# Threshold attention and a gelu feed-forward on one core: v in nine-key packets, two pairs' scores computed twice, and a planner that shares the DMA engines

## The chip, the cores and the metric

The kernel runs on one core of a Trainium2 chip. The metric is the device time of one execution in microseconds (us); the time before is the median of three executions, 1317.71 us (1317.33 to 1318.2). Five engines work side by side, each through its own list of instructions in order: TensorE (PE, matrix products, with weight loads listed apart as PEld), VectorE (DVE), ScalarE (ACT), GpSimd (POOL) and SyncE (SP), which here only issues transfers. Sixteen DMA engines move the data. Products are written to PSUM, everything else lives in SBUF; both have 128 partitions.

## The reference

```python
scores = scale * np.matmul(q, k.transpose(0, 1, 3, 2))      # (8, 8, 576, 64) each
thresh = np.max(scores, axis=-1, keepdims=True) - tau
scores = np.where(scores >= thresh, scores, -1000000000.0)
scores = scores - np.max(scores, axis=-1, keepdims=True)
attn = np.exp(scores)
attn = attn / (np.sum(attn, axis=-1, keepdims=True) + 1e-09)
x = np.matmul(attn, v)          # then (B, H, S, D) -> (B*S, H*D) = (4608, 512)
h = x @ w_in                    # w_in (512, 2048)
g = h * (1.0 / (1.0 + np.exp(-1.702 * h)))
out = g @ w_out                 # w_out (2048, 512)
```

Keys may stand in any order, as long as k and v use the same one: maximum, sum and the product with v run over all keys. In the run q, k, v and tau are 4-byte floats, while the weights w_in and w_out arrive as 8-byte floats.

## The kernel before, in words

**Tiling.** The heads of one batch are taken in pairs: batch 0 is pairs 0 to 3, and 32 pairs in all. For a pair, k and q are loaded in 32-wide blocks (`load_qk`, L366), transposed on DVE (`prep`, L477), and multiplied as four 64x64 quarters of the PE array (`scores`, L493). One tile `j` of nine holds 64 keys by 2 heads by 576 queries: keys lie along partitions, with the first half of the queries on partitions 0 to 63 and the second half on 64 to 127. ACT copies each tile from PSUM to SBUF (`keep`, L510); PSUM has three such tiles (`psA`). DVE takes the maximum over keys with a reduction that transposes (`in_groups`, L516, two key tiles at once, the ninth alone: "t" counts these five pieces), folds it over tiles (`over_tiles`, L525) and over the partition blocks less tau (`over_halves`, L536 and L542). The threshold row is then spread over partitions: for pairs in `BY_DMA` through DRAM (`turn_rows` L553, `row_out` L566, `row_in` L575), for pair 2 by a transpose (`spread_max`, L557). DVE subtracts it (`sub`, L580), ACT sends what is below to minus infinity with a very steep Prelu (`mask`, L586) and exponentiates (`exps`, L590). PE multiplies by a block of ones for the sums and by v for the result (`by_values`, L601, tiles `den` and `pv`). Pairs 0 to 4 take their sums on PE (L632), pairs 5 to 7 on DVE (`one_group`, L643 and L647), later ones on DVE with the row sent through DRAM (`turn_sums`, L658). `place_x` (L703) scales `pv` into the input of the feed-forward, and only then is the PSUM tile of `pv` free.

**Weights.** The 8-byte weights come in 32 pieces of 1 MB, by two transfers each that POOL issues (`load_w`, L428 and L429), and are turned into 4-byte floats by `cv_ex` (L439, DVE), `cv_power` (L447, ACT), `cv_frac` (L453 and L457, DVE) and `cv_end` (L465, DVE), 16 pieces of w_in and then 16 of w_out. Room for pieces not yet converted is short: a new load waits for an earlier `cv_end`. The first three pieces wait on POOL (`hold`, L484) for the transposed k of pair 2, the next three for that of pair 3.

**Stages.** Opening: pairs 0 to 3, with scores of pairs 4 and 5, and w_in. Then the first two feed-forward blocks of 256 tokens (`first_blocks`: L758 for hidden products, L764 for the gelu, L740 for the output), with pairs 4 to 9 worked in and w_out converted. Then steady work: feed-forward blocks (L718, L730, L909, L931) with one pair's attention in between; from pair 7 (`JOINT`) on a pair's scores are interleaved tile by tile with the values of the pair two before. A last stretch without attention ends it.

**What sets the order.** No order is written by hand. `task()` records each step with its engine, a cost in us, a rank, the tasks it follows, the buffers it takes and gives back, and a lag until others see it. Ranks are the pair's number plus a bias from a table by function name: `EARLY` for pairs 0 to 3, `SECOND` for 4 to 7, `LATER` for the rest, `CV` for conversions. `run_in_order()` plays the tasks through a heap of events and each engine takes the lowest-ranked task that is ready, so that the costs decide the order in which instructions are emitted. A transfer is a part of the lag of its issuing task there: fixed 10, 3 or 5.2 us and the like, whatever else moves. On the chip an engine keeps the emitted order, and waits where its next instruction is not ready.

Of the kernel before, what the change touches and what calls it, by code (L numbers as in the profile page):

```python
# [10 lines left out]
FP32 = mybir.dt.float32  # L11
# [4 lines left out]
ALU = mybir.AluOpType  # L16
# [14 lines left out]
def kernel(  # L31
# [84 lines left out]
    stop = const.tile([P, 1], FP32, name="stop")  # L116
    shift = const.tile([P, 1], FP32, name="shift")
# [9 lines left out]
    for x in ("raw0", "raw1", "qkT0", "qkT1", "mb"):  # L127
# [6 lines left out]
        "exps": -11.47,  # L134
        "in_groups": 5.75,
        "keep": 10.66,
        "load_qk": -0.27,
        "load_v": 4.86,
        "mask": -2.66,
        "one_group": -15.86,  # L140
        "one_row": 12.67,
        "over_halves": -7.01,
        "over_tiles": -4.01,
        "place_x": -17.11,
        "prep": -11.73,
        "row_in": 20.49,
        "row_out": 4.47,
        "scores_run": 12.45,
        "spread_max": -1.73,
        "spread_sums": 7.14,  # L150
        "sub": 9.27,
        "sums_by_pe": 0.27,
        "sums_in": -9.39,
        "sums_out": 2.13,
        "turn_rows": -12.55,
        "turn_sums": -0.41,
        "values": 14.64,
        "w_sum": 4.11,
        "x_sum": -14.1,
    }  # L160
    SECOND = {
        "exps": -7.29,
        "in_groups": 20.95,
        "keep": 16.67,
        "load_qk": -8.88,
        "load_v": 5.53,
        "mask": 2.36,
        "one_group": 2.55,
        "one_row": -2.71,
        "over_halves": -12.07,  # L170
        "over_tiles": 2.86,
        "place_x": -20.26,
        "prep": 3.49,
        "row_in": -19.42,
        "row_out": -24.08,
        "scores_run": -7.99,
        "spread_max": -3.11,
        "spread_sums": -2.29,
        "sub": 14.98,
        "sums_by_pe": 35.93,  # L180
        "sums_in": 7.43,
        "sums_out": 4.05,
        "turn_rows": -3.84,
        "turn_sums": 4.03,
        "values": 11.79,
        "w_sum": -10.45,
        "x_sum": -10.98,
    }
    LATER = {
        "exps": 2.01,  # L190
        "in_groups": 10.37,
        "keep": -0.02,
        "load_qk": -6.6,
        "load_v": 3.77,
        "mask": 14.79,
        "one_group": 4.78,
        "one_row": -14.98,
        "over_halves": 1.09,
        "over_tiles": -6.27,
        "place_x": -0.34,  # L200
        "prep": 2.34,
        "row_in": 4.02,
        "row_out": 2.64,
        "scores_run": -11.25,
        "spread_max": -9.44,
        "spread_sums": -6.73,
        "sub": 2.14,
        "sums_by_pe": 1.46,
        "sums_in": 3.78,
        "sums_out": 2.16,  # L210
        "turn_rows": 12.26,
        "turn_sums": 0.29,
        "values": -10.38,
        "w_sum": 6.61,
        "x_sum": 6.02,
    }
    CV = {
        "cv_end": -8.05,
        "cv_ex": 2.22,
        "cv_frac": -11.72,  # L220
        "cv_power": -4.72,
        "load_w": -7.79,
    }

    LAG = {"PE": 0.26, "DVE": 0.18, "ACT": 0.22, "POOL": 0.18}

    QUARTERS = ("scores", "scores_run", "values", "sums_by_pe")
# [12 lines left out]
    FIRST, LAST = -9.0, 1000.0  # L240
    need, follows = {}, {}

    def run_in_order():
# [7 lines left out]
        events = [(0.0, 1, i) for i, n in enumerate(left) if n == 0]  # L251
# [3 lines left out]
        mode, held_for = None, None  # L255
        while events:
            now = events[0][0]
            while events and events[0][0] <= now:
                _, kind, i = heapq.heappop(events)
                engine, _, rank, _, _, _, _, give, lag = tasks[i]  # L260
                if kind == 0:
                    busy.discard(engine)
# [1113 lines left out]
```

## Time and profile before

| | us |
|---|---|
| median of three executions | 1317.71 |
| the profiled execution, its own time | 1317.94 |
| span of the profiled execution | 1316.2 |
| PE busy / weight loads | 1260.9 / 975.6 |
| DVE, ACT, POOL busy | 1006.1, 646.6, 249.0 |
| PE busy from 0 to 118 us of the span | 77.0 |
| bytes moved | 102.88 MB in 258819 packets |
| packets under 512 bytes | 233754 |

The span runs from the first to the last recorded instruction. A group of instructions in the profile reads: line, engine, operation, output and inputs by tile name, shapes, count, busy time, mean; tile names such as `arena` cover many buffers that share one allocation. In a list of waits, "PE ps L493 <- DVE arena L477: 15.3, 3, 8.3" says that PE's instructions of line 493 stood idle for 15.3 us in 3 stalls, the longest 8.3, until DVE's line 477 was done. Fp32 products appear as two records each. In the table of stretches each engine has its busy time and, in brackets, its count.

### The profile page before, as it was taken

To read this page: it belongs to the slowest core of one execution; us is meant where nothing else is said; L and a number is where in the kernel's file an instruction comes from. 1 tells how busy PE (TensorE), PEld (TensorE's weight loads), DVE (VectorE), ACT (ScalarE), POOL (GpSimd) and SP (SyncE) were. 2 spreads that over 40 slices of the span, in tenths; PEclk is the share of its full clock that TensorE was granted. 3 is DMA by queue.
4 is the path that set the end of the run, shared out by engine and by line. 5 is a ranking of instruction groups with operands and counts; after the bars stand their busy time and mean duration, and the time that the engine had idled before them with its cause. 6 is when DMAs were issued, how large, how long until landed. Compare 5 with 4: busy or idle time off the path is not lost. (4 is left out here: it accounts for less than half of the span.)

```text
span 1316.2 us, 22807 instructions
## 1 busy us (share of the span) xinstructions
PE 1260.9 (96%) x9128; PEld 975.6 (74%) x9128; DVE 1006.1 (76%) x1610; ACT 646.6 (49%) x830; POOL 249.0 (19%) x291
## 2 busy tenths in 40 slices
PE   5669999999999999999999999999999999999998
PEld 2346864457887777777778888777777778888887
DVE  7989999898888887788777877777888863652642
ACT  4876666576554555555554555454556540210210
POOL 1201211012031211213021303030212117120120
PEclk8879999999999999999999999999999999999999
DMA  8976766545323223212213222323122110000000
GB/s 152 293 189 207 230 207 149 112 77 100 85 55 71 55 55 71 51 50 54 58 42 72 55 71 55 71 55 71 36 55 54 36 46 8 9 1 25 8 0 32
DMA packets 258819, 102.88 MB, mean 78 GB/s; under 512 B 233754, under 2 KB 243994, under 8 KB 258714
## 3 DMA queue, kind: packets, MB, share of 16 engines
q1 hardware_dynamic: 244986, 63.40, 22.4%
q0 software_dynamic: 11360, 37.74, 9.3%
q8 instruction: 71, 1.16, 0.4%
q10 hardware_dynamic: 2368, 0.30, 0.2%
q14 instruction: 34, 0.28, 0.1%
HBM read 87.51 MB, written 9.69 MB: 74 GB/s over the span
## 5 line engine op out<-in xcount | busy, mean ns | idle before, releaser
L516 DVE TRANSPOSE_TENSOR_REDUCE part<-arena 128x36 f32<-128x1152 f32 (+1 forms) x295 | 357.5, 1235 | 41.9 <-ACT arena L510 32.4
L718 PE MATMUL hps<-xT,w_in 128*128 128x256 f32 x1536 | 337.2, 380 | 0.5 <-DVE arena L730 0.4
L718 PEld LDWEIGHTS hps<-xT,w_in 128*128 128x128 f32 x1536 | 290.7, 190 | 45.9 <-issue 5.7
L586 ACT ACTIVATE arena<-arena 128x1152 f32<-128x1152 f32 (+1 forms) x160 | 169.4, 1059 | 144.0 <-DVE arena L580 143.8
L510 ACT COPY arena<-ps 128x576 f32<-128x576 f32 x288 | 170.7, 647 | 115.3 <-PE ps L493 111.9
L580 DVE TENSOR_TENSOR arena<-arena 128x1152 f32<-128x1152 f32 (+1 forms) x158 | 201.1, 1313 | 20.5 <-DMA arena<-row 20.5
L909 PE MATMUL ops<-w_out,arena 128*128 128x256 f32 x896 | 202.4, 380 | 1.8 <-DVE arena L730 1.8
L590 ACT ACTIVATE arena<-arena,shift,scl 128x1152 f32<-128x1152 f32 (+1 forms) x160 | 200.3, 1252 | 4.1
L493 PE MATMUL ps<-arena 64*64 64x288 f32 x2304 | 174.7, 420 | 22.9 <-DVE arena L477 15.3
L909 PEld LDWEIGHTS ops<-w_out,arena 128*128 128x128 f32 x896 | 169.3, 190 | 28.7 <-DVE arena L730 3.1
L875 POOL TENSOR_TENSOR arena<-arena 128x256 f32<-128x256 f32 x56 | 49.7, 888 | 647.1 <-DVE arena L730 543.9
L601 PE MATMUL pv<-arena 64*64 64x288 f32 x2176 | 159.7, 408 | 0.0
L727 ACT ACTIVATE th<-hps 128x512 f32<-128x512 f32 x112 | 66.0, 589 | 186.0 <-PE hps L718 171.8
L909 PE MATMUL ops<-arena 128*128 128x256 f32 x672 | 150.7, 380 | 0.7 <-DVE osb L931 0.7
L493 PEld LDWEIGHTS ps<-arena 64*64 64x64 f32 x2304 | 84.0, 137 | 90.8 <-ACT arena L510 30.4
L909 PEld LDWEIGHTS ops<-arena 128*128 128x128 f32 x672 | 127.1, 190 | 20.4 <-issue 2.2
L601 PEld LDWEIGHTS pv<-arena 64*64 64x64 f32 x2176 | 82.1, 134 | 54.1 <-issue 10.0
L931 DVE SCALAR_TENSOR_TENSOR osb<-ops,osb 128x256 f32<-128x256 f32 x98 | 39.3, 413 | 97.9 <-PE ops L909 90.6
L730 DVE SCALAR_TENSOR_TENSOR arena<-th,hps 128x512 f32<-128x512 f32 x96 | 64.2, 669 | 46.7 <-ACT th L727 46.4
L740 PE MATMUL ops<-w_out,arena 128*128 128x512 f32 x128 | 57.2, 600 | 3.2 <-DVE w_out L465 2.2
L758 PE MATMUL hps<-xT,w_in 128*128 128x256 f32 x256 | 56.4, 381 | 0.0
L888 POOL TENSOR_TENSOR arena<-arena 128x512 f32<-128x512 f32 x28 | 35.6, 1272 | 108.3 <-PE ops L909 108.3
(115 smaller groups left out, 1044.7 us busy)
## 6 DMA issues: line engine op xcount, KB each, us to landing
arena<-in_v_dram SPq DMA_DIRECT2D x128, 144.0 KB
arena<-in_q_dram SPq DMA_DIRECT2D x128, 72.0 KB
out_dram<-osb SPq DMA_DIRECT2D x36, 256.0 KB
arena<-in_k_dram SPq DMA_DIRECT2D x124, 72.0 KB
arena<-row SPq DMA_DIRECT2D x62, 144.0 KB
arena<-row_s SPq DMA_DIRECT2D x48, 144.0 KB
w_out<-in_moe_w_in_dram POOLq DMA_DIRECT2D x12, 512.0 KB, 9.5
arena<-in_moe_w_out_dram POOLq DMA_DIRECT2D x12, 512.0 KB, 6.3
```

The costliest lines, as they stand in the source:

```text
L493: nc.tensor.matmul(ps[ts(c, KT), h, 0:SH], lhsT=mats[n, 1][ts(h, D), ts(j, KT)], rhs=mats[n, 0][ts(h, D), ts(c, SH)], start=True, stop=True,)
L510: nc.scalar.copy(out=sT[n, t][:, u], in_=pss.pop((n, j))[:, :, 0:SH])
L516: nc.vector.tensor_reduce(out=stats[n, op][:, t * 2 * QB : min(2 * t + 2, NK) * QB], in_=sT[n, t].rearrange("p u h (g d) -> p (u h g) d", ...
L580: nc.vector.tensor_tensor(out=s, in0=s, in1=mbs[n].unsqueeze(1).to_broadcast(list(s.shape)), op=ALU.subtract)
L586: nc.scalar.activation(out=s, in_=s, func=AF.Prelu, alpha=STEEP)
L590: nc.scalar.activation(out=s, in_=s, func=AF.Exp, scale=scl, bias=shift)
L601: nc.tensor.matmul(o[c][ts(h, D), 0:SH], lhsT=left(j, h)[ts(c, KT)], rhs=sT[n, t][ts(c, KT), u, h, :], start=(j == 0), stop=(j == NK - 1),)
L718: nc.tensor.matmul(hidden[j][:, ts(f, BLK)], lhsT=w_in[:, c, ds((f * HF + j) * P, P)], rhs=xTs[blk][:, c, :], start=(c == 0), stop=(c == N ...
L727: nc.scalar.activation(out=ths[j], in_=hidden[j], func=AF.Tanh, scale=GELU_SCALE / 2)
L730: nc.vector.scalar_tensor_tensor(out=g[:, :, j, :], in0=two(ths.pop(j)), scalar=1.0, in1=two(hidden.pop(j)), op0=ALU.add, op1=ALU.mult,)
L740: nc.tensor.matmul(acc[i], lhsT=g0[:, j, ts(i, P)], rhs=w_out[:, j, :], start=(j == 0), stop=(j == NFC - 1),)
L909: nc.tensor.matmul(banks[blk][k][:, ts(o, HM)], lhsT=left[:, j, :], rhs=right[:, j, :], start=(j == 0), stop=(j == HF - 1),)
```

## The change

**v.** `load_v` reads nine consecutive keys of v into one partition, so that 64 pieces of 2304 bytes take the place of 576 of 256 bytes in each transfer. Key tile `j` then holds every ninth key. For k, `load_qk` loads the blocks in the order that gives the same set of keys, its pieces keep their 128 bytes.

**Scores twice.** For pairs 2 and 3 (`TWICE`) the copied scores are used for the maximum alone. `over_halves` writes the thresholds with all four partition blocks, `row_blocks` transposes them and multiplies by a mask `own_row`, so that each of 64 partitions has the thresholds of its own queries and zero elsewhere. `again` computes the scores a second time and adds to the same PSUM tile a product of that matrix with `minus`, a block of minus ones. `mask_one` is the Prelu straight from PSUM to SBUF. `sub` and `mask` fall away for these two pairs.

**Sums.** Pairs 5 to 7 send their sums through DRAM as the later ones do (`SUMS_BY_DMA` from 5).

**The planner.** A transfer is a task of its own on one of two movers, `DMS` for what SP and ACT issue and `DMW` for POOL's weights. Where both are busy they share: small packets (kind 0) get 0.055 of the engines, larger ones (kind 1) 0.3, the weights the rest. The biases of all tables are new, and the costs of conversions and of SP's issues are changed. `BY_POOL`, which would give some subtractions to POOL, is empty. Four memsets, a fill by position and their constants stand at the program's start on POOL, ahead of the load of tau.

```diff
-        "exps": -11.47,
-        "in_groups": 5.75,
...
+        "again": -31.04,
+        "exps": -25.04,
+        "in_groups": 37.12,
...
+    MOVERS = ("DMS", "DMW")
+    SHARE = (0.055, 0.3)
+    def transfer(by, time, a, kind=0, give=(), lag=1.7):
+        return task(by, time, FIRST, moved, kind, after=[a], give=give, lag=lag)
...
+        def rates():
+            if len(flow) < 2:
+                return dict.fromkeys(flow, 1.0)
+            x = SHARE[tasks[flow["DMS"][0]][4][0]]
+            return {"DMS": x, "DMW": 1.0 - x}
...
+    TWICE = (2, 3)
+    BY_POOL = {}
...
+                rows = src[b, 2 * hp + h, :, ts(j, 32)]
                 queue.dma_start(
                     out=blocks[ds(64 * h + 32 * j, 32), :, :],
-                    in_=src[b, 2 * hp + h, :, ts(j, 32)].rearrange("(c p) d -> p c d", p=32),
+                    in_=rows.rearrange("(a p t) d -> p t a d", a=2, p=32) if which
+                    else rows.rearrange("(c p) d -> p c d", p=32),
                 )
...
-                    out=t[ts(c, KT), :, h, :],
-                    in_=v[b, 2 * hp + h].rearrange("(j k) d -> k j d", k=KT),
+                    out=t[ts(c, KT), h],
+                    in_=v[b, 2 * hp + h].rearrange("(k j) d -> k j d", k=KT),
...
+        if n in TWICE:
+            for x, y in ((0, 0), (1, 2), (2, 1), (3, 3)):
+                nc.vector.scalar_tensor_tensor(
+                    out=flat[0][ts(y, 32), 0:QB], in0=r[ts(x, 32)], scalar=gap[ts(x, 32)],
+                    in1=o[ts(x, 32)], op0=ALU.subtract, op1=ALU.max,
+                )
+            return
...
+    def row_blocks(n):
+        nc.vector.transpose(out=flat[1], in_=flat[0])
+        mb = home(n, "mb")[:, 0:SH]
+        nc.vector.tensor_tensor(
+            out=mb.rearrange("p (g i) -> p g i", i=32),
+            in0=flat[1].unsqueeze(1).to_broadcast([P, QB // 2, 32]),
+            in1=own_row.unsqueeze(2).to_broadcast([P, QB // 2, 32]), op=ALU.mult,
+        )
+        mbs[n] = mb
+
+    def again(n, j):
+        ps = psA.tile([P, 2, 512], FP32, name="ps", tag="ps")
+        for first in (True, False):
+            for h in range(2):
+                for c in range(2):
+                    if first:
+                        left = mats[n, 1][ts(h, D), ts(j, KT)]
+                        right = mats[n, 0][ts(h, D), ts(c, SH)]
+                    else:
+                        left, right = minus[ts(h, D), c, :], mbs[n][ts(h, D), :]
+                    nc.tensor.matmul(
+                        ps[ts(c, KT), h, 0:SH], lhsT=left, rhs=right, start=first, stop=not first,
+                    )
...
+    def mask_one(n, j):
+        nc.scalar.activation(
+            out=sT[n, j // 2][:, j % 2], in_=pss.pop((n, j))[:, :, 0:SH], func=AF.Prelu, alpha=STEEP
+        )
...
+    nc.gpsimd.memset(minus, 0.0)
+    nc.gpsimd.memset(own_row, 0.0)
+    for x in range(4):
+        nc.gpsimd.memset(minus[ts(x, 32), x % 2, :], -1.0)
+        nc.gpsimd.affine_select(
+            out=own_row[ts(x, 32)], in_=own_row[ts(x, 32)], compare_op=ALU.not_equal, fill=1.0,
+            base=-(QB // 2) * (x // 2), pattern=[[-1, QB // 2]], channel_multiplier=1,
+        )
...
-    BY_PE = 5
-    BY_DMA = (0, 1, *range(3, NP))
-    SUMS_BY_DMA = range(8, NP)
+    SUMS_BY_PE = (0, 1, 2, 3, 4)
+    BY_DMA = (0, 1, *range(4, NP))
+    SUMS_BY_DMA = range(5, NP)
...
-        cost = 3.5 if NPAIR <= n < 2 * NPAIR else 2.0
-        lag = (4.6, 3.0)[n] if n < 2 else 10.0 if n < 2 * NPAIR else 3.0
...
+        lq, lk = (transfer("DMS", 1.45, a, lag=1.7 if n else 3.2) for a in (lq, lk))
...
+            if n in TWICE:
+                for j in range(2 * t, min(2 * t + 2, NK)):
+                    m = task(
+                        "PE", 0.97 * slow, r, again, n, j, after=[m], take=("psA",),
+                        give=own(n, "qkT0", "qkT1", "mb") if j == NK - 1 else (),
+                    )
+                    a = task("ACT", 0.62, r, mask_one, n, j, after=[m] + mx, give=("psA",))
+                ws.append(task("ACT", 0.76 if tail else 1.24, r, exps, n, t, after=[a]))
+                continue
```

## The prediction

> **What bounds the kernel now.** I read the page's first part, then the engines by stretch, then what TensorE waited for.
>
> ```profile
> PE 1260.9 (96%) x9128; PEld 975.6 (74%) x9128; DVE 1006.1 (76%) x1610; ACT 646.6 (49%) x830; POOL 249.0 (19%) x291
> ```
>
> The span is 1316.2, so TensorE (PE) lacks 55.3 us. By stretch (columns: length, busy PE, weight loads, DVE, ACT, POOL, then clock, DMA share, GB/s):
>
> ```profile
> 20.00:40.00 20.00, 7.07 (x76) 3.94 (x80) 19.54 (x27) 9.28 (x14) 6.87 (x14) 0.73 0.86 249
> 40.00:60.00 20.00, 15.64 (x214) 8.71 (x211) 19.66 (x35) 19.41 (x19) 3.20 (x6) 0.92 1.04 326
> 60.00:80.00 20.00, 10.05 (x152) 4.82 (x144) 18.78 (x29) 15.45 (x21) 4.23 (x8) 0.84 0.87 248
> 118.00:180.00 62.00, 62.00 (x411) 50.43 (x410) 59.88 (x102) 32.59 (x43) 13.39 (x24) 1.00 0.72 232
> 180.00:280.00 100.00, 93.58 (x631) 45.54 (x630) 93.25 (x150) 68.66 (x86) 7.42 (x10) 0.98 0.55 123
> 330.00:1100.00 770.00, 766.38 (x5676) 611.76 (x5675) 611.80 (x929) 400.54 (x500) 152.86 (x158) 1.00 0.25 56
> ```
>
> Of the 55.3 us, 41 lie before 118, where VectorE (DVE) is all but full, 6.4 in 180 to 280, 0.8 in 280 to 330, 3.6 in the 770 us of steady work, 3.2 at the end. So two places are for sale. The waits of PE, first up to 118, then from 118 to 340:
>
> ```profile
> PE ps L493 <- DVE arena L477: 15.3, 3, 8.3
> PE den L601 <- DVE r L632: 12.9, 2, 10.8
> PE den L601 <- DVE w_out L457: 7.0, 1, 7.0
> ```
>
> ```profile
> PE ps L493 <- ACT arena L510: 3.6, 4, 2.2
> PE ops L740 <- DVE w_out L465: 2.2, 2, 1.6
> PE ops L740 <- DVE arena L764: 0.9, 1, 0.9
> ```
>
> The opening waits on DVE. Its marks are the first subtraction, the last placement of batch 0, and PE's first feed-forward product (timeline, start and length):
>
> ```profile
> 34.67 2.63 DVE L580 TENSOR_TENSOR arena<-arena 128x1152 f32<-128x1152 f32 x2 [0.23 <-DMA arena<-row]
> 114.40 0.95 DVE L703 TENSOR_TENSOR xT<-pv,arena 128x256 f32<-128x256 f32 x4
> ```
>
> ```profile
> 117.60 1.99 PE L758 MATMUL hps<-xT,w_in 128*128 128x256 f32 x8
> ```
>
> After 117.6 PE runs to the end. In both programs' order the same PE work stands after that product (scores of six pairs, sums and values of four stand before it), 1184 us. So the new time follows from two things: when this product starts, and PE's idle time after it (14.2 us).
>
> **What the Trainium skill says.** DMA: Bandwidth & Descriptors, Queues, rings and completion order: each DMA engine alternates between queues by packet. The trace agrees that queues hurt each other: SP's four loads of one k beside POOL's weights took 10.8 us to issue (169.59), against 2.1 alone. Same page, Why small descriptors are slow: a fixed cost per packet; the trace has 200 GB/s for v's 256 B packets (10 to 12.5 us), about 140 for the 128 B ones of q and k, 400 for weights. TensorE: Matmul & The Clock Gate, What's actually happening: an idle PE falls to half clock; the trace shows 0.50 from 76 to 84. VectorE: DVE Perf Modes, The TRN2 errata: ScalarE takes (224+n)/1.2 ns from SBUF, (172+n)/1.2 from PSUM; for n=576 667 and, by estimate, 623. The trace has 670 for the first, 652 for a copy from PSUM. I take 650 for the new Prelu from PSUM.
>
> **The change part by part.**
> *Scores twice.* Per pair nine tiles of 16 PE records more; eight records cost 0.485 (11.57 us for 144 is slower only because ACT frees the banks). So 0.97 x 18 = 17.5 us, by cold clock up to 25. It lies before 117.6, in 41 us of idle PE. If that cover were gone it would cost all 17.5.
> DVE loses ten subtractions: 8 x 1.26 + 2 x 0.67 = 11.4 us (start to start). It gains, per pair, eight 32-row operations at 0.26 plus transpose 0.14 and a 128x288 product at about 0.42 (256 wide: 0.424), less the old threshold steps: for both pairs +2.0.
> ACT: nine Prelus at 0.65 for 4 x 1.18 + 0.68, +0.5 a pair, not on the path.
> *Reordering.* Counting DVE's instructions up to the last placement: changed program 11.4 subtractions, 16.1 maxima over groups, 1.4 over tiles, 5.3 thresholds of the twice-scored pairs, 15 x 1.4 + 15 x 0.65 conversions (30.8), 12.6 sums and placements, 2.7 transposes: 80.3 us from the first subtraction. The old count is 74.7, measured 80.6 with 5.9 idle (3.7 of it for a threshold row). So what is saved is filled by two to three more weight pieces (4.8) and pair 4's maxima (6.3). Walking ACT beside it, DVE waits about 3 us for copies. Last placement: 83.3 after the first subtraction, before: 80.6.
> *First subtraction.* It waits for pair 0's threshold row. The SP queue, start and issue time:
>
> ```profile
> 23.50 0.86 SPq L566 DMA_DIRECT2D row<-flat  x2
> 26.20 1.13 SPq L575 DMA_DIRECT2D arena<-row  x2
> 28.77 0.75 SPq L566 DMA_DIRECT2D row<-flat  x2
> 35.48 1.40 SPq L575 DMA_DIRECT2D arena<-row  x2
> ```
>
> The row came back 7.3 us after its issue ended, beside weights; alone 2.3 (85.98 to 88.3). In the new order both v loads stand ahead of q and k of pairs 2, 3, and v1 no longer between k3 and the row: SP's sum is the same, row out at about 23. But k2's transpose comes at 20.7, not 25.1, and releases POOL's weights, flowing from about 23 instead of 27, while k3 (issued 20.4 to 22.5) and the row still move. If k3 gets through, the row goes in at 25 and lands 7.3 after 26.4: 33.7. If k3 is caught: 36 to 39. DVE is ready at 31.6 (three maxima fewer ahead). I take 34.0; bounds 31.6 and 39. Last placement 34.0 + 83.3 = 117.3, two us later than before; but then PE waited 2.3 after it for scores now done, so the first product is at 117.6 again: **0**, bounds -3 and +5.
> *After it* DVE has 14.7 us less: 11.1 done ahead (4.8 + 6.3) and 1.2 for each of three pairs whose sums go by DMA (1.35 in place of 1.4 for the fold and 1.15 for reciprocal and spread). The 2.2 us for late w_out and the 3.6 for copies behind a full DVE shrink; 0.95 (first output product waits for a bank) stays. Take -5.2 and put 1.0 back for the longer sums chain: **-4.2**, bounds -6.5 and +3.
> *v in packets of nine keys.* 128 issues of 576 packets of 256 B become 64 of 2304 B: 65,536 packets fewer. Landing was never on PE's path; SP's issue (0.66 each) is not shorter. 0; if v had been late, up to -1, in the bounds above. Four more memsets, a mask and a library switch on POOL stand ahead of tau: the switch shows 0.675 us at 284.1, at most 5.3 fits there. Tau landed at about 5.3, is used at 9.2: 0, at worst 2 in the bound above.
> *Steady state.* New ranks, 3.6 us idle in 770: nothing to win, up to +2 to lose.
> Sum: 0 - 4.2. The profiled execution's own time is 1317.94, its span 1316.2, so 1.7 lies around it; the median is 1317.71, 0.2 lower. 1317.7 - 4.2 = 1313.5.
>
> **Rivals.**
> *Slower: weights starve k3 and the row.* One mechanism, at 23 to 32 us: k3's small packets and pair 0's row share engines with weights that now start 4 us earlier, and DVE, in order, stands at k3's transpose with every maximum of pair 1 behind it, and PE's sums and ACT's exponentials behind those. For: 7.3 against 2.3 us above. Against: k3 has 1 to 3 us before the flow is full. The first subtraction at 39 puts the first product at 122.6, +5, less 1 to 2 regained: 1321. It decides from a first subtraction at about 38.2.
> *No difference.* ACT becomes the bound: from the first mask to the last exponential of pair 3 it has 22.6 + 23.4 + 7.2 of copies + 7.7 of conversions = 60.9, then 12.6 more before the first product: 34 + 1.3 + 73.5 = 108.8 without a wait. Eight us of room; alternation of PE, ACT and PE in the twice-scored pairs may eat them. With the start 2 to 3 later and -3 regained: 1317.
> *The extra scores aren't hidden.* PE's 77 us before 118 become 94.5; if PE's order forced them behind each other from 33 on, start +10: 1324. Against: DVE needs all the time to 117 anyway.
>
> **How the numbers follow.** A tell-from-none bound of 0.2% is 2.6 us. Forecast 1313.5, chance 0.50, its own range 1308 to 1315; no difference 0.19; starving 0.24; unhidden scores or a late steady state 0.07. Range for eight in ten: 1307 (both lower bounds nearly met) to 1322 (the starving case in full). Faster 0.50, same 0.19, slower 0.31.
>
> **What would show it.** Right: PE before the first product about 94 us busy, that product at 115 to 120; the first subtraction at 32 to 36; no PE wait on w_out in 180 to 280; idle after the product near 10. Wrong: DVE idle before k3's transpose or the first subtraction over 4 us; ACT above 19 of 20 us from 60 to 110; new PE waits on exponentials; idle above 5 us in the steady stretch.

## The result and the profile after

| | before | after |
|---|---|---|
| median, us | 1317.95 (1317.33 to 1323.53) | 1333.16 (1330.6 to 1334.97) |
| ratio | | 1.0104, 95% interval 1.0072 to 1.0136 |
| span of the profiled execution, us | 1316.2 | 1331.4 |
| first feed-forward product at, us | 117.60 | 133.98 |
| span after that product, us | 1198.6 | 1197.4 |
| packets | 258819 | 194098 |

The forecast was 1313.5 us, faster. The kernel became 1% slower, and the time lies beyond the range's upper end of 1322. A ratio and its interval are estimated from all executions of a kernel and of the kernel before, timed beside it, so that it need not be the quotient of the two medians shown. In the spans of the profiled executions all of the loss, and 1.2 us more, lies before the first feed-forward product. The same views as before, of the changed kernel. The first part of the page:

```profile
PE 1274.5 (96%) x9416; PEld 984.2 (74%) x9416; DVE 989.4 (74%) x1600; ACT 638.0 (48%) x838; POOL 243.9 (18%) x301
```

TensorE works 13.6 us more, VectorE 16.7 us less. By stretch (columns as before: length, busy PE, weight loads, DVE, ACT, POOL, then clock, DMA share, GB/s):

```profile
20.00:40.00 20.00, 6.79 (x80) 3.18 (x76) 9.28 (x15) 6.58 (x12) 5.18 (x12) 0.75 0.74 208
40.00:60.00 20.00, 11.18 (x116) 5.88 (x120) 19.73 (x27) 14.56 (x15) 1.60 (x4) 0.57 0.49 172
60.00:80.00 20.00, 16.82 (x268) 10.07 (x264) 19.16 (x41) 15.70 (x20) 4.45 (x8) 1.00 0.48 108
118.00:180.00 62.00, 56.71 (x443) 43.36 (x436) 56.13 (x103) 30.18 (x40) 14.70 (x26) 0.94 0.82 241
180.00:280.00 100.00, 93.66 (x610) 51.69 (x612) 86.65 (x139) 62.16 (x79) 7.46 (x10) 0.97 0.55 128
330.00:1100.00 770.00, 765.18 (x5774) 608.45 (x5773) 608.34 (x937) 398.92 (x505) 138.16 (x153) 1.00 0.24 57
```

Look at the first line: VectorE, the engine that sets the opening's pace, works 9.28 of 20 us; it was 19.54. VectorE's timeline says why (start, length, and in brackets the idle time before and what ended it; the transposes at 22.45 and 37.03 are those of k of the third pair and of the fourth, the one at 122.87 is that of k of the sixth; the subtraction is the first, the placement the last):

```profile
22.45 0.78 DVE L531 STREAM_TRANSPOSE arena<-arena 128x576 f32<-128x576 f32 x1
...
37.03 0.78 DVE L531 STREAM_TRANSPOSE arena<-arena 128x576 f32<-128x576 f32 x1 [10.42 <-DMA arena<-in_k_dram]
...
43.96 5.12 DVE L675 TENSOR_TENSOR arena<-arena 128x1152 f32<-128x1152 f32 x4
...
114.38 0.44 DVE L507 TENSOR_SCALAR w_out<-w_out 128x512 int32<-128x512 int32 x1 [2.74 <-DMA w_out<-in_moe_w_in_dram]
...
122.87 0.78 DVE L531 STREAM_TRANSPOSE arena<-arena 128x576 f32<-128x576 f32 x1 [1.51 <-DMA arena<-in_k_dram]
...
132.24 0.95 DVE L798 TENSOR_TENSOR xT<-pv,arena 128x256 f32<-128x256 f32 x4
```

VectorE stands 10.42 us for k of the fourth pair. The first subtraction falls 9.3 us later than before, the last placement 17.8 us. SyncE's queue, start and length of issue:

```profile
22.43 2.67 SPq L419 DMA_DIRECT2D arena<-in_k_dram  x4
25.19 1.16 SPq L660 DMA_DIRECT2D row<-flat  x2
36.85 1.14 SPq L669 DMA_DIRECT2D arena<-row  x2
```

That k was issued by 25.1 us and came at 37.0; the row, two transfers of 2.2 KB, was issued by 26.4 us and let its return be issued only at 36.85. In between POOL had six weight transfers under way, issued from 23.9 to 27.1 us. That row and k are done within 0.2 us of each other is no accident of this run: with k in time (run 1 below) the two marks are 26.66 and 26.70. It suggests that the row, issued last, stood behind k in SyncE's own queue, so that the weights held up one queue and not two transfers apart; no run separates the two. What the DMA engines did from 25.1 to 36.9 us (queue, packets, MB, share of the sixteen engines' time; q0 is POOL's, q1 SyncE's):

```profile
q0 software_dynamic: 672, 3.14, 78.9%
q1 hardware_dynamic: 1274, 0.16, 8.8%
```

The weights took nine times the engine time of SyncE's queue, which needed all of these 11.8 us for 0.16 MB: what was left of k, and the row. What TensorE waited for up to 134 us, and then up to 340:

```profile
PE den L696 <- ACT arena L685: 19.9, 3, 18.9
PE ps L547 <- DVE neg L1063: 10.1, 1, 10.1
PE ps L547 <- DVE arena L531: 6.6, 2, 4.4
```

```profile
PE ps L547 <- ACT arena L564: 6.6, 2, 6.3
```

The 10.1 us are the wait for the first score product, at the program's start (8.3 before). The 18.9 us stall is the echo of VectorE's: no subtraction, no exponential, no sums. The waits for w_out after 180 us are gone, as forecast, but one stall of 6.3 us has come in their place.

### The profile page after: what moved, and what is told of

Same layout as the page of the kernel before. It is cut to its first block, busy times and chain, and to the rows that moved or that the text cites. A ratio compares the mean times of both kernels' runs of the same rounds, so it can differ in the third digit from the quotient of the medians.

```text
span 1331.4 us, 23379 instructions
## 1 busy us (share of the span) xinstructions
PE 1274.5 (96%) x9416; PEld 984.2 (74%) x9416; DVE 989.4 (74%) x1600; ACT 638.0 (48%) x838; POOL 243.9 (18%) x301
## 2 busy tenths in 40 slices
DMA packets 194098, 103.53 MB, mean 78 GB/s; under 512 B 160198, under 2 KB 171206, under 8 KB 193990
## 4 chain that ended last, share of the span: by engine, by line
PE 79%; DVE 7%; ACT 6%; DMA 4%; SPq 2%; issue 2%; POOL 0%; DVEq 0%; ACTq 0%
PE ops L1004 24%; PE hps L813 21%; PE pv L696 9%; PE ps L547 8%; PE ps L918 4%; PE hps L853 4%; PE ps L1004 4%; PE ops L918 3%; ACT arena L685 2%; DMA arena<-in_k_dram 2%; DVE part L570 2%; ACT arena L681 2%; SPq L419 2%; DVE arena L675 1%; DMA w_out<-in_moe_w_in_dram 1%
## 5 line engine op out<-in xcount | busy, mean ns | idle before, releaser
L681 ACT ACTIVATE arena<-arena 128x1152 f32<-128x1152 f32 (+1 forms) x150 | 155.7, 1060 | 174.1 <-DVE arena L675 173.8
L675 DVE TENSOR_TENSOR arena<-arena 128x1152 f32<-128x1152 f32 (+1 forms) x149 | 184.3, 1267 | 32.0 <-DMA arena<-row 32.0
L685 ACT ACTIVATE arena<-arena,shift,scl 128x1152 f32<-128x1152 f32 (+1 forms) x160 | 195.7, 1248 | 1.6
L531 DVE STREAM_TRANSPOSE arena<-arena 128x576 f32<-128x576 f32 x64 | 46.0, 747 | 25.4 <-DMA arena<-in_k_dram 15.4
```

The source lines that it names most:

```text
L675: engine.tensor_tensor(out=s, in0=s, in1=mbs[n].unsqueeze(1).to_broadcast(list(s.shape)), op=ALU.subtract)
L681: nc.scalar.activation(out=s, in_=s, func=AF.Prelu, alpha=STEEP)
L685: nc.scalar.activation(out=s, in_=s, func=AF.Exp, scale=scl, bias=shift)
```

## The experiments

**Theory:** weights released 2.5 us earlier (23.4 us) and k issued 3.8 us later (from 22.4 us) than before meet; the small packets of k and of the threshold row starve (first meeting: their packets get little of the DMA engines beside the weights), and the same happens again near 105 to 120 us to k of the sixth pair (second meeting). **Rivals:** the scores made twice are on the path; the planner's new order is long by itself; the new form of the loads costs something.

In the kernels built on the changed one, the emitted order was recorded and kept, and only the named tasks were moved in it. A cure is an edit that undoes one suspected cause.

**1. Weights wait for k of the fourth pair (e1_hold_k3).**

```diff
+        at = next(x for x, i in enumerate(order) if tasks[i][3] is prep and tasks[i][4] == (3, 1))
+        late = [i for i in order[:at] if tasks[i][3] in (hold, load_w)]
...
+        return rest[: at + 1] + late + rest[at + 1 :]
...
-        nc.gpsimd.tensor_copy(out=stop, in_=held_k[n][:, 0:1])
+        nc.gpsimd.tensor_copy(out=stop, in_=held_k[3][:, 0:1])
```

> The changed kernel in its own order; only the first wait of the weights is moved, from k of the third pair to k of the fourth, so that the first six weight transfers leave GpSimd after k of the fourth pair has been transposed. Theory A, the weights starve k of the fourth pair and the first threshold row: k is transposed near 29 us without a wait for its transfer, the first subtraction falls to 34-37 us (43.96 in the changed kernel), the first feed-forward product to 120-127 us (133.98), the time to 1319-1327 us. Theory B, the reordered work and the scores made twice are what is late: the first subtraction stays over 41 us, the product over 131 us, the time at 1331-1336 us. If only the first collision is cured and the second (k of the sixth pair, near 120 us) is not, the product comes near 125 us and not below.

Measured: 1326.61 us, ratio to before 1.0072 (1.0057 to 1.0087). VectorE's timeline, the transpose of that k and the first subtraction:

```profile
26.70 0.78 DVE L541 STREAM_TRANSPOSE arena<-arena 128x576 f32<-128x576 f32 x1 [0.70 <-DMA arena<-in_k_dram]
...
33.62 2.59 DVE L685 TENSOR_TENSOR arena<-arena 128x1152 f32<-128x1152 f32 x2
```

and the row's return on SyncE's queue, with what this queue moved from 24.7 us, the end of k's issue, to 26.7:

```profile
26.66 1.14 SPq L679 DMA_DIRECT2D arena<-row  x2
```

```profile
q1 hardware_dynamic: 1281, 0.16, 50.6%
```

Without weights beside it the queue moves as many packets in 2.0 us as it did in 11.8. The wait for k falls from 10.42 to 0.70 us, the first subtraction comes 1 us earlier than before the change. The first product moves to 125.22, still 7.6 us late: the expectation's theory B, that the reordered work and the second scores are what is late, is out for the first subtraction, but something else remains.

**2. The same on the kernel before, the other way round (b_early).** The first three pieces are released by the first pair's threshold row, 6 us earlier; nothing else changes.

```diff
+        late = [i for i in order if tasks[i][3] is hold and tasks[i][4] == (2,)]
+        late += [i for i in order if tasks[i][3] is load_w][:3]
...
+        return rest[: at + 1] + late + rest[at + 1 :]
...
-        nc.gpsimd.tensor_copy(out=stop, in_=held_k[n][:, 0:1])
+        nc.gpsimd.tensor_copy(out=stop, in_=flat[1][:, 0:1] if n == 2 else held_k[n][:, 0:1])
```

> The kernel before, with nothing but the first three weight pieces released some 6 us earlier: they wait for the first pair's transposed thresholds (near 19.5 us), not for k of the third pair (25.9 us), so that they run beside k of the fourth pair and the first threshold row. Theory A: k of the fourth pair lands near 33 us (transposed at 28.67 before, with no wait), the first subtraction moves from 34.67 to 39-44 us, the first feed-forward product from 117.60 to 121-127 us and the time to 1322-1328 us. Theory B (starvation is not what costs): the first subtraction stays below 37 us and the time is 1315-1320 us.

Measured: 1327.32 us, ratio 1.0083 (1.0062 to 1.0104); first product at 124.94. SyncE's queue and VectorE's timeline:

```profile
18.61 2.06 SPq L376 DMA_DIRECT2D arena<-in_k_dram  x4
20.71 9.93 SPq L387 DMA_DIRECT2D arena<-in_v_dram  x4
30.74 3.03 SPq L576 DMA_DIRECT2D row<-flat  x2
```

```profile
37.21 0.21 DVE L563 STREAM_TRANSPOSE flat<-flat 128x32 f32<-128x32 f32 x1 [8.68 <-DMA row<-flat]
37.35 0.75 DVE L487 STREAM_TRANSPOSE arena<-arena 128x576 f32<-128x576 f32 x1
...
43.06 2.58 DVE L590 TENSOR_TENSOR arena<-arena 128x1152 f32<-128x1152 f32 x2
```

The early weights alone cost the kernel before 0.8%, and move its first subtraction from 34.67 to 43.06, much as in the changed kernel. The victim is another one: the issue of v took 9.93 us in place of 2.65, the row stood behind it in SyncE's queue, and VectorE waited to overwrite the row's source.

**3. v of the first two pairs behind k of the fourth (e_v_late)**, weights released where the changed kernel does.

```diff
+        vs01 = [i for i in order if tasks[i][3] is load_v and tasks[i][4][0] < 2]
...
+        return rest[: at + 1] + vs01 + rest[at + 1 :]
```

> The changed kernel in its own order, but on SyncE the v of the first two pairs (eight loads) is issued behind k of the fourth pair instead of ahead of q of the third. All else, the place where the weights are released included, stays. Theory A with v as its cause: q and k of the third and fourth pairs are issued some 4.5 us earlier; k of the third pair then also lands earlier and releases the weights earlier (20-21 us instead of 23.4), so that only part is gained: k of the fourth pair transposed at 30-35 us instead of 37.0, the first subtraction at 36-42 us, the time 1324-1332 us. If the order on SyncE alone were at fault, the first subtraction would be back at 34-36 us and the time at 1320-1325 us. Theory B: 1331-1336 us.

Measured: 1330.95 us, ratio 1.011 (1.0087 to 1.0132). SyncE's queue, then VectorE's first subtraction:

```profile
16.48 3.25 SPq L428 DMA_DIRECT2D arena<-in_k_dram  x4
19.77 5.45 SPq L440 DMA_DIRECT2D arena<-in_v_dram  x8
25.32 1.35 SPq L669 DMA_DIRECT2D row<-flat  x2
34.80 1.10 SPq L678 DMA_DIRECT2D arena<-row  x2
```

```profile
43.01 5.17 DVE L684 TENSOR_TENSOR arena<-arena 128x1152 f32<-128x1152 f32 x4 [7.53 <-DMA arena<-row]
```

The time is as expected (though by itself it hardly differs from theory B's 1331), the way to it is not: k was to be transposed at 30 to 35 us and the subtraction to come by 42. k is in time (transposed at 25.17 without a wait), but k of the third pair releases the weights 1.2 us sooner (22.2 us), and the row takes the late k's place among them, now behind v's eight loads in SyncE's queue: out at 26.7 us, back at 43. In this run the order on SyncE changes which small transfer suffers, and the loss stays.

**4. The second meeting (e1_v4).** To cure 1, v of the fifth pair moves behind q and k of the sixth.

```diff
+        v4 = next(i for i in order if tasks[i][3] is load_v and tasks[i][4][0] == 4)
...
+        return order[: at + 1] + [v4] + order[at + 1 :]
```

> The kernel of e1_hold_k3 (weights released by k of the fourth pair) with one more move on SyncE: v of the fifth pair, whose load stands in the queue until v of the third pair has been used, goes behind q and k of the sixth pair, which stood behind it and were issued at 98.4-112.9 us beside the weight pieces of 94-97 us. Theory A': the 90.8 us from the first subtraction to the last placement (80.6 before) are long because of this second meeting. Then q and k of the sixth pair are issued by about 85 us, TensorE's 3.94 us wait for the transposed k at 115.8 us goes, as does VectorE's 1.35 us wait for that transfer, the first feed-forward product comes at 119-122.5 us (125.22 in e1_hold_k3, 117.60 before), the time is 1320-1324 us. Rival: the order itself is what is long: the product stays over 124 us and the time at 1325-1328 us.

Measured: 1319.91 us, ratio 1.0015 (1.0004 to 1.0026); first product at 121.05, was 125.22. TensorE's wait for the transposed k fell from 3.94 to 1.45 us, VectorE's for that k from 1.35 to 0.75. The product fits theory A' and the time misses its range by 0.1 us, but neither wait is gone, and SyncE's queue shows that q and k were issued only at

```profile
95.67 7.34 SPq L433 DMA_DIRECT2D arena<-in_q_dram  x4
103.11 6.37 SPq L433 DMA_DIRECT2D arena<-in_k_dram  x4
```

not by 85 us: 2.7 and 4.1 us sooner than in run 1 (98.37 and 107.18), and still slowly, beside the weight pieces issued from 93.1 to 96.3 us. They take the seats (the buffers for loads) that q and k of the fifth pair leave when VectorE transposes them, and those transposes stand at 94.91 and 96.40 in the new order, with no wait before them; in the kernel before the first of them stands at 84.09, and q of the sixth pair went out at 86.08. The planner's place for two transposes thus sends the next loads in among those weight pieces. v of the fifth pair in front of them, waiting for its own seat, made it worse, and only that part was undone here. Whether the planner put the transposes there because the second scores hold q and k longer wasn't tried; on the chip the third pair's second scores were done by 79.2 us.

**5. The form of the loads.** On top of 4, k and v are loaded as before. Beside it, on the kernel before, both new forms (e2_v_alone), then k's alone and v's alone; in these last two the keys of k and v don't pair.

```diff
-                rows = src[b, 2 * hp + h, :, ts(j, 32)]
...
-                    in_=rows.rearrange("(a p t) d -> p t a d", a=2, p=32) if which
-                    else rows.rearrange("(c p) d -> p c d", p=32),
+                    in_=src[b, 2 * hp + h, :, ts(j, 32)].rearrange("(c p) d -> p c d", p=32),
```

> The kernel of e1_v4 with the loads of k and v written as before (keys in order, v in packets of one key), all else the same. If the new form of k's load, whose four issues took 2.67 us where the old one's took 2.06, is a cost of its own (e2_v_alone was 1.0031 of the kernel before), this one is 2-4 us faster than e1_v4: 1317-1322 us, with the first transposed k some 0.7 us earlier. If the cost in e2_v_alone came only from where it pushed the threshold row among the weights, and v's larger packets pay for it here, it is equal to e1_v4 or 1-2 us slower.

> The kernel before with only the packets changed: v in packets of nine keys, q's columns as they were, k's columns in the matching order; every instruction stays at its place. Both theories: v is never what a value product waits for before 118 us, so 1315.5-1318.5 us; fewer packets might free the transfer engines beside the weights and take up to 2 us. A rival that blames the new layout of k's load or of v's: more than 1320 us.

> The kernel before with nothing but the new form of k's load (keys split in two halves, 32 lanes and nine neighbours; v keeps its order, so that keys and values don't pair as they should). If k's load is what made e2_v_alone 1.0031 of the kernel before: four issues of k take 2.7 us on SyncE instead of 2.06, k of the second pair is waited for near 11.1 us, the first subtraction comes at 36-38 us (34.67 before), the time at 1319-1322 us. If v's packets were the cause: 1316.5-1318.5 us.

> The kernel before with nothing but the new form of v's load and its matching reads (packets of nine keys; k keeps its order, so that keys and values don't pair as they should). If k's load is the cause of e2_v_alone's loss, this one is 1315.5-1318 us, not slower than before, and its first subtraction stays at 34-35.5 us; if v's form costs by itself: 1319-1321 us.

| | us | ratio to before, 95% |
|---|---|---|
| e1_v4_old | 1316.86 | 0.9988 (0.9973 to 1.0004) |
| e2_v_alone | 1320.56 | 1.0031 (1.0018 to 1.0044) |
| k_form | 1322.39 | 1.0026 (1.0014 to 1.0039) |
| v_form | 1317.2 | 0.9990 (0.9979 to 1.0002) |

v's packets cost nothing that can be told, k's new form does: four issues take 2.7 us in place of 2.06, on SyncE's queue, ahead of everything else. k_form's queue and the subtraction it leads to:

```profile
19.88 2.68 SPq L366 DMA_DIRECT2D arena<-in_k_dram  x4
...
28.01 1.39 SPq L576 DMA_DIRECT2D arena<-row  x2
```

```profile
38.21 2.63 DVE L581 TENSOR_TENSOR arena<-arena 128x1152 f32<-128x1152 f32 x2 [3.57 <-DMA arena<-row]
```

Three k loads add under 2 us, which push the row's return from 26.20 to 28.01, deeper among the weights: it lands 3.5 us later (34.67 to 38.21). The expectation for e2_v_alone, 1315.5 to 1318.5, was missed; k_form and e1_v4_old lie 0.4 and 0.1 us outside theirs.

With the weights held back, k's form acts elsewhere. Of the 2.0 us by which the span of e1_v4_old is shorter than that of e1_v4, only 0.3 lie before the first product (120.74 for 121.05); behind it the stall near 250 us is 4.38 us in place of 6.57. How k's form reaches that stall was not followed.

**6. Are the extra scores hidden (half_again)?** In e1_v4_old the products that subtract the threshold are left out.

```diff
-        for first in (True, False):
+        for first in (True,):
...
-                        ps[ts(c, KT), h, 0:SH], lhsT=left, rhs=right, start=first, stop=not first,
+                        ps[ts(c, KT), h, 0:SH], lhsT=left, rhs=right, start=True, stop=True,
```

> The kernel of e1_v4_old with the second half of every repeated score left out: the 18 groups of four products that subtract the threshold in PSUM, 18 times 0.485 = 8.7 us of TensorE's work (so the thresholds of two pairs are not subtracted); every other instruction keeps its place. The prediction's step b, that these are hidden in TensorE's idle time before the first feed-forward product: the product moves by less than 1.5 us from 120.7 us and the time stays at 1314.5-1318 us. Rival, the extra scores are on the path: the product comes 6-9 us earlier and the time is 1308-1311 us.

Measured: 1316.9 us, ratio 0.9991 (0.9983 to 0.9999), against 1316.86 and 0.9988 with them. TensorE up to the first product, in e1_v4_old and here (same columns as the stretches):

```profile
0.00:120.70 120.70, 90.02 (x1296) 52.60 (x1296) 101.87 (x187) 85.51 (x118) 20.65 (x53) 0.93 0.79 203
```

```profile
0.00:119.30 119.30, 82.60 (x1152) 47.07 (x1152) 101.79 (x187) 85.04 (x118) 20.33 (x53) 0.91 0.80 204
```

7.4 us less work move the product by 1.4 us and the time by nothing that can be told. So this half of the extra work is hidden but for 1.4 us; the other half, the scores computed again, was not taken out.

**7. One part alone, planned anew.** On the kernel before: the scores twice, and the sums by DMA, each with the old tables. The first brings the code of the second scores with it.

```diff
+    TWICE = (2, 3)
...
```

```diff
-    SUMS_BY_DMA = range(8, NP)
+    SUMS_BY_DMA = range(5, NP)
```

> The kernel before with nothing but the scores of the third and fourth pair made twice with their thresholds in PSUM, ordered by the planner and the tables of before. The prediction's step b: the 17.5 us that TensorE has more are hidden in its idle time before the feed-forward products, VectorE is relieved of the subtractions of two pairs, some 11 us of it in the early part: the first product at 108-118 us, the time 1308-1318 us. The rival 'extra scores not hidden': TensorE is busy some 94 us of the time before the product and this starts 6-17 us later, the time 1324-1335 us. A weight release or a row that this order shifts can add some us to either; the wait is then seen on VectorE before the first subtraction.

> The kernel before with the sums by DMA from the sixth pair on instead of from the ninth, ordered by the planner and the tables of before. Up to 180 us almost nothing moves. The prediction's step e says that this takes some of VectorE's work out of 180-280 us, where TensorE waits 6.4 us: between 0 and 4 us faster, 1312.5-1317 us. Rival: two more round trips through DRAM come late beside weights and the time is 1317-1320 us.

Measured: 1337.02 us, ratio 1.0137 (1.0106 to 1.0167), and 1331.68, ratio 1.0106 (1.0082 to 1.013). Neither expectation of b_sums was met, and b_twice is slower than even its rival said. They can't be read as the price of the parts, nor do they clear the second scores, for the planner made another order of everything: in b_sums the first product is at 118.40, but from 180 to 330 us VectorE waits for transfers,

```profile
DVE arena L477 <- DMA arena<-in_q_dram: 10.4, 1, 10.4
DVE arena L580 <- DMA arena<-row: 4.8, 1, 4.8
```

and TensorE is 14 us less busy there than before; in b_twice the product is at 126.64 and one wait of 10.5 us follows at 257.3. What they show is that in these two cases the old tables didn't carry over to other tasks.

**8. The late stall (t_sum_late).** On e1_v4_old, one block sum of the weights (two negations on ACT, then an accumulating 1 MB transfer by POOL) is moved away from the eighth pair's row.

```diff
+        t2 = [i for i in order if tasks[i][3] in (t_minus, t_plus) and tasks[i][4][0] == 1]
...
+        return order[: at + 1] + t2 + order[at + 1 :]
```

> The kernel of e1_v4_old with one block sum of the weights moved: ScalarE's two negations (225.1 us there) and GpSimd's accumulating 1 MB transfer behind them (227.4 us) go behind the fourth copy of the ninth pair's scores (near 248 us). In e1_v4_old that transfer leaves beside the eighth pair's threshold row, which VectorE awaits for 2.33 us at 234.7 us, and TensorE then stands 4.38 us at 247.7 us for ScalarE. If this third meeting and ScalarE's 2 us before it are what stalls TensorE: the row lands by about 232 us, the wait falls from 4.38 to 0.5-1.5 us, the time to 1312.5-1314.5 us. Rival, the stall has another cause or comes back behind the moved transfer at the next row: 1316-1318 us.

Measured: 1315.92 us, ratio 0.9991 (0.998 to 1.0003). VectorE's subtraction for that row, in e1_v4_old and here:

```profile
234.73 5.83 DVE L687 TENSOR_TENSOR arena<-arena 128x1152 f32<-128x1152 f32 x5 [2.33 <-DMA arena<-row]
```

```profile
231.50 5.80 DVE L691 TENSOR_TENSOR arena<-arena 128x1152 f32<-128x1152 f32 x5
```

The row is in time and TensorE's stall falls from 4.38 to 1.29 us, as expected. The span after the first product is 1193.5 us, against 1194.9; some of the gain comes back as waits of 1.4 us at 187.8 and 0.9 at 288.5. The time is above the 1312.5 to 1314.5 expected and can't be told from e1_v4_old.

**9. Reordered keys without k's slow form?** Eighteen neighbouring keys a lane (a partition of the load's target) for k; v either with a matching split of its lanes (first two runs), or as in v_form, with the pairing made by the transpose's output order (last two).

```diff
+                        "(p c) d -> p c d" if which else "(c p) d -> p c d", p=32
...
+                    in_=v[b, 2 * hp + h].rearrange("(p a j) d -> a p j d", a=2, p=32),
```

```diff
+        out = dst.rearrange("q (t p a) -> q a t p", a=2, p=32) if which else dst
+        nc.vector.transpose(out=out, in_=raws.pop((n, which)))
```

> The kernel before with v in packets of nine keys and keys paired as in the changed kernel's idea, but k loaded with 18 neighbouring keys a lane, so that its pattern has one dimension fewer; the transpose on VectorE reads the blocks in the order that pairs them with v. If the cost of e2_v_alone (1.0031) and k_form (1.0026) is the extra dimension of k's pattern, four issues of k take 2.1 us again, the first subtraction comes at 33.5-35.5 us and the time is 1315.5-1318 us, like v_form (0.9990). If reordered keys cost whatever the pattern, by slower reads or a slower transpose: 1319-1322 us.

> The kernel of t_sum_late (weights released by k of the fourth pair, v of the fifth pair behind k of the sixth, one block sum of weights later, k and v loaded as before) with v in packets of nine keys and k with 18 neighbouring keys a lane. If v's larger packets free the engines beside the weights and k's form is free: 1313-1315.5 us (0.997-0.999 of the kernel before), the first feed-forward product at 118.5-119.8 us. If v's packets bring nothing: 1315.5-1317 us. If k's order costs: 1318 us or more.

> The kernel before with k in 18 neighbouring keys a lane, v exactly as in v_form, and the pairing made by the transpose's output order. k18_before (1.1399) kept the DMA engines at 0.29 of their time from 8 to 24 us, near two of sixteen, behind the first v; so v's pattern with an outermost dimension of two is suspected there, not k's. If so, the queue is free again and only k's issue (2.6-3.0 us for four in k18_before, no shorter than in k_form) is left: 1317-1322 us, the first subtraction at 35-38 us. If k's 18 neighbouring keys, or the transpose's order, were what clogged: over 1400 us.

> The kernel of t_sum_late with k in 18 neighbouring keys a lane, v as in v_form and the pairing made by the transpose's output order. With k's issue still at 2.6 us and v's packets as cheap as in v_form (0.9990): 1315-1319 us, between t_sum_late (0.9991) and e1_v4 (1.0015). Under 1315 us if v's packets pay beside the weights of the mended order; over 1400 us if k's order clogs the engines.

| | us | ratio to before, 95% |
|---|---|---|
| k18_before | 1502.77 | 1.1399 (1.1373 to 1.1424) |
| k18_t_sum | 1562.63 | 1.1852 (1.1827 to 1.1878) |
| k18_v9_before | 1319.05 | 1.0009 (0.9996 to 1.0022) |
| k18_v9_t_sum | 1315.37 | 0.9980 (0.9970 to 0.9989) |

The first two were a plain miss. The busy share of the sixteen DMA engines from 8 to 24 us, in tenths, in 40 slices of 0.4 us, first in the kernel before, then in k18_before:

```profile
DMA  7993586998999999999989987600877888749899
```

```profile
DMA  5945690101175111111113111148111111291111
```

Behind the first v, issued from 8.9 to 11.3 us, the engines are at a tenth in most slices (0.29 over the whole, 0.85 before), and q behind it takes 11.9 us to issue. The Trainium skill, DMA: Bandwidth & Descriptors, Rules for kernel authors, says that an outermost dimension smaller than 16 keeps the whole transfer on that many engines at most; v's pattern had a 2 there. The runs agree: two of sixteen engines would be 0.125, and with v's lanes unsplit the same k costs nothing that can be told (1.0009). The transpose differs as well between these runs, but takes 0.73 to 0.78 us in both. k's issue stays at 2.6 us for four, so that the idea of a cheaper pattern failed; why this form costs less than k_form, with an issue as long, was not found, and the intervals overlap. The last kernel, with the cures of runs 1, 4 and 8 and larger v packets, is the only one here that leaves nothing out and is faster than the kernel before: by 0.2%, with an interval that excludes no change.

## Why the prediction was wrong

**What bounds the kernel: right.** The opening waits on VectorE, and the first feed-forward product carries the end: the product moved by 16.4 us and the span by 15.2. The product had been forecast where it was, at 117.6. Of the 16.4 us, 10.0 are the first subtraction (43.96 for 34.0), 5.9 the stretch from there to the last placement, 0.5 the step from there to the product. (A slip in the sum of TensorE's idle time: the end has 3.4 us and not 3.2. Nothing hangs on it.)

**The first subtraction: the step that failed.** "If k3 gets through, the row goes in at 25 ... If k3 is caught: 36 to 39. I take 34.0." It was caught, and the upper bound was too low: 43.96. I had priced being caught by the row's 7.3 us beside weights, once. In truth k takes 11.9 us from the end of its issue, that end comes 2.6 us later than I had it, and 6.9 us of transpose, maxima and thresholds stand on VectorE from this k to the first subtraction (37.03 to 43.96). The row's way back, issued at 36.85, is hidden behind them. The Trainium skill's alternation by packet, which the prediction cited (DMA: Bandwidth & Descriptors, Queues, rings and completion order), fits this mechanism, with 672 packets of weights and 1274 of SyncE's moved together, but gives no price for it. The case was written down as the rival "weights starve k3 and the row", with its right mechanism and place, at a chance of 0.24 and at 1321; even its price was 12 us short, for it took the subtraction at 39 and no second meeting. Its argument against, that k has "1 to 3 us before the flow is full", assumed that k's issue ends at 22.5. It ended at 25.1, because v's eight issues and the longer issues of k stand ahead, and by then the flow was 1.2 us old.

**"SP's sum is the same": wrong.** Four issues of k take 2.67 us, not 2.06. The step "v in packets of nine keys: 0" missed it, since it counted v's issues and not those of k, whose pattern the same step had changed. Alone that form made the kernel before 1.0026 times as long.

**First subtraction to last placement: 83.3 forecast, 89.2 measured** (from start to end, 43.96 to 133.19). VectorE's work in that stretch is 78.6 us (I had counted 80.3; the old stretch, counted as 74.7, holds 73.5); the idle time is 10.6 and not 3. Of it 5.2 is for weight pieces and k of the sixth pair and 1.5 for sums behind them: the second meeting, which the prediction didn't look for. With the cures of runs 1 and 4 and the old loads the stretch takes 86.8 (e1_v4_old), still 3.5 over the forecast.

**Extra scores hidden: right as far as tested.** TensorE is 92.6 us busy before the product (94 forecast), and run 6 shows the cover for half of the extra work.

**After the product: -4.2 forecast, -1.2 measured.** The waits for w_out went as said. In their place came the 6.3 us stall at 262 us, behind a row that left beside the accumulating weight transfer (238.2). TensorE's idle time after the product is 15.4 us, where near 10 had been named as a sign of being right. In run 8, with the row out of the transfer's way and the old loads, the span after the product is 1193.5 us, 5.1 less than before (1193.5 in k18_v9_t_sum too): the size was about right, but what the row would meet wasn't looked at.

**ACT as the bound, the steady state, POOL's additions at the start:** of the stretches before the product ACT's busiest is 17.8 of 18 us, from 100 to 118, close to full but behind VectorE's delays; the steady 770 us have 4.8 us idle against 3.6, inside the +2; POOL's additions, six memsets and four fills by position, hold the load of tau back by 1.5 us (2.91 for 1.39), and the first subtraction of run 1, at 33.62, leaves no visible cost of it.

In spans, the ladder from the changed kernel down is 1331.4, 1325.1 (weights behind k), 1317.6 (v behind q and k), 1315.6 (old form of the loads), against 1316.2 before, and in ratios 1.0104, 1.0072, 1.0015, 0.9988: undoing the three brings the time back to what it was. It does not bring the product back: in e1_v4_old it starts at 120.74, 3.1 us later than before, and a shorter part behind it makes up for that (1194.9 for 1198.6). VectorE's work before the product is the same there as in the kernel before (101.9 and 101.7 us), so that what the change saves there is filled by other work, as the prediction had said, and nothing is gained. Whether the 3.1 us are the planner's order or what is left of the second scores isn't shown. Left open too: why the part after the product varies by some 3 us between runs 1 and 4 while their order there is the same (1199.9 and 1196.6). Each is one execution, and executions of the kernel before alone spread from 1314.3 to 1324.4 us in run 4's series.

## What to carry over

When an edit moves the release of a large transfer, list every small transfer that is issued from there until the large one has landed, and price each of them at its time beside the flood, one after the other where one waits for the other; here a release 2.5 us earlier and an issue 4 us later were worth 9 us on the first subtraction. Count issue time anew for each pattern that changes, and look up which instruction frees the seat of each load, since the load can't leave before it. Don't count on an order tuned by a model of costs when the tasks or the transfers change: in run 7 two such changes cost over 1% each.

## What the runs showed of the hardware that I had not expected

- A load in 128-byte packets beside three weight pieces of 1 MB crawls: the last 0.16 MB of k and the row took 11.8 us, with 8.8% of the engines' time against 78.9% for the weights; without weights as much took 2.0 us (run 1). For the row issued behind k, two transfers of 2.2 KB, 10.5 us pass from the end of its issue to the start of its return's, where before the change 1.8 us passed.
- The order of a load's addresses changes its issue time: 0.515 us for one of k as before (2.06 for four), 0.67 with two halves and nine neighbours, 0.65 with eighteen neighbours, at equal bytes and packets.
- A split of v's lanes into an outermost dimension of two made the whole kernel 14% slower (1.1399, against 1.0009 with the lanes unsplit).
